# Decode attention on one core: Q loaded plainly and transposed on TensorE instead of by transposing DMAs, with a new fixed loop order and deeper buffers

## The chip, the cores and the metric

The kernel runs on one core of one Trainium2 chip. The metric is the device time of one execution in microseconds (us), lower being better. Each execution also has a span (first to last instruction) and the mean clock that TensorE was granted. Most executions of one kernel agree within about 0.3%, except for a rare slow state in which the granted clock is far lower; such a run is left out of comparisons.

## The reference

Grouped-query attention, with 4 query heads for each key/value head, all in bf16:

```python
B, Hq, Hkv, Sq, Sk, D = 16, 32, 8, 16, 2048, 128      # q: B,Hq,Sq,D   k, v: B,Hkv,Sk,D
k = jnp.repeat(k, 4, axis=1)
v = jnp.repeat(v, 4, axis=1)
scores = jnp.einsum("bhqd,bhkd->bhqk", q, k) * D ** -0.5
p = softmax(scores, axis=-1)
return jnp.einsum("bhqk,bhkd->bhqd", p, v)
```

For each of the 128 groups (one batch, one key/value head) 64 query rows meet 2048 keys. K and V are 67 MB each, and each byte is used for one group only, so the loads weigh about as much as the computing.

## The kernel before

Two groups make a *pair* (2 x 64 = 128 query rows), and the kernel is one unrolled pipeline over 64 pairs. For a pair p:

- SyncE issues loads of K and V (512 KB a group, rows of 4 KB to each partition), of Q, and the store of an earlier pair.
- TensorE (PE) transposes K in four blocks of eight 128x128 tiles (`KT`), each into one of three staging banks of PSUM (`ST_ps`); a copy (`kte`) takes each bank to SBUF.
- PE computes the scores (`S`) into `S_ps`, of which there is one; VectorE (DVE) scales them, takes the maximum and moves them to SBUF (`max`); ScalarE (ACT) does the exponential (`exp`).
- PE transposes P in two blocks (`PT`), copies (`pte`) take them out, PE multiplies by V (`PV`), and a last pass divides by the row sum (`norm`).

Each engine's program is a list made in Python. The parts that the change and the argument touch:

```python
NBK = 8; NBV = 12; NBO = 8      # slots for K, V and the output
DV = 2; DSTORE = 7              # V is issued 2 pairs after K, the store 7
QCH = 512                       # query rows in one load of Q: 16 loads

for kk in range(0, last_std + 1):                 # PE
    if kk < NP:  pe_prog.append(("S", kk))
    if kk >= 1:  pe_prog.append(("PT", kk - 1))
    pe_kt(kk)                                     # all four blocks of K of pair kk + 2
    if kk >= 1:  pe_prog.append(("PV", kk - 1))
# ... DVE: recip(kk-1), max(kk), all four K copies of pair kk + 2
# ... ACT: both P^T copies of kk-1, exp(kk), norm(kk-1)
# ... the last three pairs have an order of their own (`tail`)

def issue_q(c):
    sp.dma_start_transpose(QT[:, qch * c:qch * (c + 1)],
                           qf[qch * c:qch * (c + 1), :]).then_inc(sem_q[c], 16)

def issue_k(g):
    s = g % NBK
    if g >= NBK:                                  # slot free once its transposes are done
        ld = kt_loads[((g - NBK) // 2, (g - NBK) % 2, 1)]
        sp.wait_ge(sem_stage, ld["u"] + 1)
    sp.dma_start(Kn[s][:, :, :], k[b, h].rearrange("(a j) d -> a j d", j=J)).then_inc(sem_k[s], 16)

# PE, before transposing K: a load is there when all 16 increments are
pe.wait_ge(sem_k[s], 16 * (g // NBK + 1))
```

## Time and profile before

| before | value |
|---|---|
| median of the 12 runs beside the result | 380.04 us (379.74 to 380.91) |
| span of the profiled run, granted clock | 378.6 us, 0.995 |
| busy: PE, VectorE, ScalarE | 325.3, 307.9, 272.6 us |
| bytes moved by the queue of loads and stores | 138.43 MB |
| turn (start of one maximum to the next), steady | 5.60 us |

The columns are line, engine, operation, output and input, count; then busy time and mean nanoseconds; then the idle time just ahead of these instructions and what ended it.

```profile
L374 DVE TENSOR_SCALAR_CACHE_REDUCE Sneg<-S_ps 128x2048 f32<-128x2048 f32 x64 | 146.7, 2291 | 55.1 <-PE S_ps L312 55.1
L364 DVE COPY KT<-ST_ps 128x1024 bf16<-128x1024 bf16 x254 | 157.9, 683 | 7.9 <-PE ST_ps L300 7.7
```

VectorE stands idle for 55.1 us ahead of its maxima, waiting for scores: 64 x 0.86 us, the hole in each turn. It hardly waits for K's transposes (7.9 us).

### The profile page before, as it was taken

What the parts mean: (1) busy time and instruction counts of PE and PEld (TensorE: products, weight loads), DVE (VectorE), ACT (ScalarE), POOL (GpSimd) and SP (SyncE); (2) the same over time, 40 slices, a digit from 0 to 9 for tenths busy, and PEclk for the clock granted to TensorE, in tenths of its full rate; (3) what the DMA queues carried; (4) which work ended last, traced back from release to release, by engine and by line L of the source; (5) the groups of instructions that cost most, each with busy time, mean ns of one, the idle gap of its engine ahead of it and who ended that gap; (6) DMA issues with size and microseconds to landing.
All of it is one profiled execution on the core that took longest, in us unless ns stands there. A gap on an engine that the chain in (4) does not pass through costs nothing.

```text
span 378.6 us, 12914 instructions
## 1 busy us (share of the span) xinstructions
PE 325.3 (86%) x5632; PEld 257.0 (68%) x5632; DVE 307.9 (81%) x453; ACT 272.6 (72%) x316; POOL 1.0 (0%) x6
## 2 busy tenths in 40 slices
PE   4779889889888988988889889888988988988884
PEld 3567667677676776776677676776776776776664
DVE  2968888888898898797888898898898887898675
ACT  1457877777787787686877787787787786787882
POOL 1000000000000000000000000000000000000000
PEclk9989999999999999999999999999999999999999
DMA  8999999999999999999999999999999999999950
GB/s 256 346 407 345 407 404 351 410 346 409 355 399 413 345 402 347 410 406 346 412 344 407 366 394 408 348 412 348 406 411 346 406 342 412 406 409 409 409 204 12
DMA packets 54839, 139.25 MB, mean 368 GB/s; under 512 B 22016, under 2 KB 22016, under 8 KB 54784
## 3 DMA queue, kind: packets, MB, share of 16 engines
q1 hardware_dynamic: 54784, 138.43, 100.4%
q8 instruction: 45, 0.74, 0.8%
q14 instruction: 10, 0.08, 0.1%
HBM read 134.22 MB, written 2.10 MB: 360 GB/s over the span
## 4 chain that ended last, share of the span: by engine, by line
PE 54%; ACT 29%; DMA 9%; issue 3%; SPq 2%; DVE 1%
ACT PT L394 28%; PE O_ps L343 16%; PE ST_ps L300 16%; PE S_ps L312 13%; DMA Kn<-in_k_dram 9%; PE ST_ps L328 9%; SPq L234 1%; SPq L243 1%; DVE PT L364 1%; ACT KT L394 1%; DVE Sneg L374 0%; SPq L251 0%; DVE O L385 0%
## 5 line engine op out<-in xcount | busy, mean ns | idle before, releaser
L374 DVE TENSOR_SCALAR_CACHE_REDUCE Sneg<-S_ps 128x2048 f32<-128x2048 f32 x64 | 146.7, 2291 | 55.1 <-PE S_ps L312 55.1
L300 PE MATMUL ST_ps<-ident,Kn 128*128 128x128 bf16 x2048 | 147.1, 221 | 44.0 <-ACT PT L394 33.1
L394 ACT ACTIVATE PT<-ST_ps 128x1024 bf16<-128x1024 bf16 x124 | 120.1, 1021 | 66.1 <-PE ST_ps L328 66.1
L364 DVE COPY KT<-ST_ps 128x1024 bf16<-128x1024 bf16 x254 | 157.9, 683 | 7.9 <-PE ST_ps L300 7.7
L300 PEld LDWEIGHTS ST_ps<-ident,Kn 128*128 128x128 bf16 x2048 | 119.5, 99 | 65.4 <-issue 31.0
L398 ACT ACTIVATE P<-Sneg,nbias 128x2048 bf16<-128x2048 f32 x64 | 128.2, 2003 | 10.9 <-DVE Sneg L374 10.9
L328 PEld LDWEIGHTS ST_ps<-ident,P 128*128 128x128 bf16 x1024 | 57.4, 98 | 26.5 <-issue 25.2
L343 PE MATMUL O_ps<-Vb,PT 128*64 128x128 bf16 x2048 | 70.5, 222 | 4.6 <-ACT PT L394 1.9
L328 PE MATMUL ST_ps<-ident,P 128*128 128x128 bf16 x1024 | 68.5, 220 | 0.5 <-ACT KT L394 0.4
L343 PEld LDWEIGHTS O_ps<-Vb,PT 128*64 128x64 bf16 x2048 | 59.9, 111 | 11.9 <-DVE PT L364 2.6
L312 PE MATMUL S_ps<-KT,QT 128*64 128x512 bf16 x512 | 66.1, 379 | 1.9 <-DVE KT L364 1.0
L409 ACT ACTIVATE O<-O_ps,rrec 128x128 bf16<-128x128 f32 x61 | 22.4, 368 | 21.1 <-PE O_ps L343 21.1
L312 PEld LDWEIGHTS S_ps<-KT,QT 128*64 128x64 bf16 x512 | 25.9, 110 | 15.2 <-issue 2.4
L398 ACT ACTIVATION_READ_ACCUMULATOR P<-Sneg,nbias 128x1 f32 x64 | 12.8, 200 | 0.0
L368 DVE RECIPROCAL rrec<-rowsum 128x1 f32<-128x1 f32 x64 | 9.8, 154 | 3.2 <-ACT P L398 3.2
L374 DVE DVE_READ_ACCUMULATOR Sneg<-S_ps 128x1 f32 x64 | 5.3, 83 | 0.0
L385 DVE TENSOR_SCALAR O<-O_ps,rrec 128x128 bf16<-128x128 f32 x3 | 1.0, 349 | 2.5 <-PE O_ps L343 2.5
L394 ACT ACTIVATE KT<-ST_ps 128x1024 bf16<-128x1024 bf16 x2 | 1.9, 1020 | 1.3 <-PE ST_ps L300 1.3
L364 DVE COPY PT<-ST_ps 128x1024 bf16<-128x1024 bf16 x4 | 2.6, 686 | 0.1
L398 ACT ACT_TABLE_LOAD x1 | 1.3, 1283 | 0.7 <-PEq L424 0.7
L229 POOL TENSOR_SCALAR ident<-iota_t 128x128 bf16<-128x128 int32 x1 | 0.5, 536 | 0.1
L227 POOL IOTA iota_t<- 128x128 int32 x1 | 0.2, 235 | 0.4 <-POOLq L424 0.4
(4 smaller groups left out, 0.4 us busy)
## 6 DMA issues: line engine op xcount, KB each, us to landing
Kn<-in_k_dram SPq DMA_DIRECT2D x128, 512.0 KB, 13.0
Vb<-in_v_dram SPq DMA_DIRECT2D x128, 512.0 KB, 12.8
out_dram<-O SPq DMA_DIRECT2D x64, 32.0 KB, 12.6
QT<-in_q_dram SPq DMA_TRANSPOSE x16, 12.3
```

The lines of the kernel that those rows point to most:

```text
L234: sp.dma_start_transpose(QT[:, qch * c:qch * (c + 1)], qf[qch * c:qch * (c + 1), :]).then_inc(sem_q[c], 16)
L243: sp.dma_start(Kn[s][:, :, :], k[b, h].rearrange("(a j) d -> a j d", j=J)).then_inc(sem_k[s], 16)
L300: ins = pe.transpose(stage_ap(ld["bank"], t), Kn[s][:, j, :], ident[:, :])
L312: ins = pe.matmul(S_ps[64 * gg:64 * (gg + 1), 512 * c:512 * (c + 1)], QT[:, 128 * p + 64 * gg:128 * p + 64 * (gg + 1)], kt[:, gg, 4 * c:4 ...
L328: ins = pe.transpose(stage_ap(ld["bank"], t), P[p % 2][:, 128 * j:128 * (j + 1)], ident[:, :])
L343: ins = pe.matmul(O_ps[64 * gg:64 * (gg + 1), 0:128], pt[:, j, 64 * gg:64 * (gg + 1)], Vb[g % NBV][:, j, :], start=(j == 0), stop=(j == J ...
L364: dve.tensor_copy(evac_dst(ld), stage_bank_ap(ld["bank"])).then_inc(sem_ev["dve"], 1)
L368: dve.reciprocal(rrec[:, p:p + 1], rowsum[:, p:p + 1]).then_inc(sem_rec, 1)
L374: dve.tensor_scalar(Sneg[kk % 2][:, :], S_ps[:, :], -scale, None, op0=ALU.mult, op1=ALU.min, accum_out=nbias[:, kk:kk + 1],).then_inc(sem_ ...
L394: act.activation(evac_dst(ld), stage_bank_ap(ld["bank"]), ACT.Copy).then_inc(sem_ev["act"], 1)
L398: act.activation(P[kk % 2][:, :], Sneg[kk % 2][:, :], ACT.Exp, bias=nbias[:, kk:kk + 1], scale=-1.0, accum_out=rowsum[:, kk:kk + 1],).then ...
L409: act.activation(Osb[s_][:, :], O_ps[:, 0:128], ACT.Copy, scale=rrec[:, p:p + 1]).then_inc(sem_nm["act"], 1)
```

## The change

The intent: take the transposing loads away from the DMA engines, which are full, and put the work on PE and ScalarE, which are not; and order the loop so that VectorE's own work sets its turn. The diff, cut to its core:

```diff
-NBK = 8;  NBV = 12; NBO = 8;  DV = 2; DSTORE = 7; QCH = 512
+NBK = 12; NBV = 16; NBO = 12; DV = 3; DSTORE = 9; QCH = 1024; NPT = 2
+    for p in range(-4, NP + 4):
+        if (p + 2) % 8 == 0 and (p + 2) // 8 < NP // 8:
+            put(pe, "QT", (p + 2) // 8)
+        put(pe, "KT", p, 0)
+        put(pe, "PV", p - 3)
+        put(pe, "KT", p + 1, 1)
+        put(pe, "PT", p - 2)
+        put(pe, "S", p)
+        put(dve, "pte", p - 2, 1)
+        put(dve, "max", p)
+        put(dve, "recip", p - 1)
+        put(dve, "kte", p + 2, 1, 0)
+        put(dve, "kte", p + 2, 1, 1)
+        put(dve, "pte", p - 1, 0)
+        put(act, "exp", p)
+        if (p + 4) % 8 == 0 and (p + 4) // 8 < NP // 8:
+            put(act, "qte", (p + 4) // 8)
+        put(act, "kte", p + 2, 0, 0)
+        put(act, "kte", p + 2, 0, 1)
+        put(act, "norm", p - 1)
 ... (the old lists and the special tail are gone; exp also waits for the transposes of P two pairs back)
             def issue_q(c):
-                sp.dma_start_transpose(QT[:, qch * c:qch * (c + 1)], qf[qch * c:qch * (c + 1), :]).then_inc(sem_q[c], 16)
+                if c >= 2:
+                    sp.wait_ge(sem_stage, q_loads[c - 2]["u"] + 1)
+                sp.dma_start(Qn[c % 2][:, :, :], qf[qch * c:qch * (c + 1), :].rearrange("(a j) d -> a j d", j=8)).then_inc(sem_q[c], 16)
 ... PE:
+                elif op[0] == "QT":
+                    pe.wait_ge(sem_q[c], 16)
+                    wait_bank_free(ld)
+                    for t in range(8):
+                        ins = pe.transpose(stage_ap(ld["bank"], t), Qn[c % 2][:, t, :], ident[:, :])
 ... ScalarE copies that bank into QT with a strided view
```

## The prediction

> **What bounds the kernel now.** I read the page's busy table first. Nothing computing is full.
>
> ```profile
> PE 325.3 (86%) x5632; PEld 257.0 (68%) x5632; DVE 307.9 (81%) x453; ACT 272.6 (72%) x316; POOL 1.0 (0%) x6
> ```
>
> VectorE needs 307.9 us, 70 us less than the span, so a sum of work on one of these engines is not what sets the end. Next the queue table and the slices:
>
> ```profile
> DMA  8999999999999999999999999999999999999950
> GB/s 256 346 407 345 407 404 351 410 346 409 355 399 413 345 402 347 410 406 346 412 344 407 366 394 408 348 412 348 406 411 346 406 342 412 406 409 409 409 204 12
> ...
> q1 hardware_dynamic: 54784, 138.43, 100.4%
> ```
>
> The DMA engines are full from the first slice to the 38th; 138.43 MB pass in that time. But the rate is not steady: it is 402 to 413 GB/s in one slice and about 345 in the next. Cutting the span into 6 us windows (last two columns: DMA share, GB/s) shows what the dips are:
>
> ```profile
> 298.00:304.00 6.00, 5.67 (x98) 4.30 (x95) 5.03 (x10) 4.55 (x6) 0.00 (x0) 1.00 1.02 406
> 304.00:310.00 6.00, 5.05 (x89) 4.04 (x90) 5.16 (x10) 4.68 (x7) 0.00 (x0) 1.00 1.14 306
> ...
> 322.00:328.00 6.00, 5.39 (x97) 4.36 (x97) 5.16 (x9) 4.68 (x6) 0.00 (x0) 1.00 1.04 412
> 328.00:334.00 6.00, 5.39 (x99) 4.36 (x96) 5.16 (x9) 4.68 (x6) 0.00 (x0) 1.00 1.03 408
> ```
>
> About one window in four falls to some 306 to 325 GB/s while its DMA share rises: the engines take longer over fewer bytes. The Q chunks come at the same rate, one per four pairs, and the last dip (304 to 310) lies a queue's latency after the last one is issued at 297.6 us; behind it the rate stays at 408 to 412.
>
> ```profile
> Kn<-in_k_dram SPq DMA_DIRECT2D x128, 512.0 KB, 13.0
> ...
> QT<-in_q_dram SPq DMA_TRANSPOSE x16, 12.3
> ```
>
> So one transposing load of Q costs (409 - 309) / 409 x 6 = 1.45 us of all 16 engines. Checked on the whole: 138.43 MB at 409 GB/s is 338.5 us; the stream runs from about 2.2 to 364.4 us, 362.2 us; the surplus of 23.7 us over 16 transposes is 1.48 us each. Both ways agree.
>
> The second bound is the compute loop. The chain of waits is mostly compute:
>
> ```profile
> PE 54%; ACT 29%; DMA 9%; issue 3%; SPq 2%; DVE 1%
> ACT PT L394 28%; PE O_ps L343 16%; PE ST_ps L300 16%; PE S_ps L312 13%; DMA Kn<-in_k_dram 9%; PE ST_ps L328 9%; SPq L234 1%; SPq L243 1%; DVE PT L364 1%; ACT KT L394 1%; DVE Sneg L374 0%; SPq L251 0%; DVE O L385 0%
> ```
>
> and the timeline of VectorE in the middle shows its turn:
>
> ```profile
> 200.73 2.29 DVE L374 TENSOR_SCALAR_CACHE_REDUCE Sneg<-S_ps 128x2048 f32<-128x2048 f32 x1 [0.84 <-PE S_ps L312]
> 202.94 0.08 DVE L374 DVE_READ_ACCUMULATOR Sneg<-S_ps 128x1 f32 x1
> 202.94 2.48 DVE L364 COPY KT<-ST_ps 128x1024 bf16<-128x1024 bf16 x4
> 205.34 0.15 DVE L368 RECIPROCAL rrec<-rowsum 128x1 f32<-128x1 f32 x1
> 206.33 2.29 DVE L374 TENSOR_SCALAR_CACHE_REDUCE Sneg<-S_ps 128x2048 f32<-128x2048 f32 x1 [0.84 <-PE S_ps L312]
> ```
>
> A pair takes 206.33 - 200.73 = 5.60 us, with 0.84 us in which VectorE waits for the scores. The ring behind it, added up from the chain in order of time: two P^T evictions on ScalarE 1.95, hand-over 0.14, the second half of the K transposes 1.05, P·V 1.01, scores 0.86, first P transposes 0.57, hand-over 0.02: 5.60. The DMA needs 362.2 / 64 = 5.66 us per pair. Two limits stand within 1% of each other, and removing either alone would win little. Last come 14.2 us of tail, from the end of the loads (364.4) to the end (378.6).
>
> **What the Trainium skill says.** "DMA: Bandwidth & Descriptors", section "Latency and other measured facts", gives the DMA transpose 261 GB/s, 350 to 400 when contiguous. This trace does not agree: a Q chunk is 131 KB, worth 0.32 us at 409 GB/s, and took 0.32 + 1.45 us, some 74 GB/s. The same page, section "iDMA fabric", has a load stream of 4 KiB rows on a core alone at 408.7 GB/s; the undisturbed windows show 406 to 412, so I take 409 as the ceiling. "TensorE: Matmul & The Clock Gate", section "PE-mode transpose", says that the transpose leaves its result in PSUM and needs a copy after it; in the trace eight K transposes are issued in 0.45 us and each bank costs a copy of 683 ns on VectorE or 1021 ns on ScalarE. "PSUM — Partial Sum Buffer", section "PSUM bank collisions raise a hardware error", asks that a bank be guarded by semaphores against write and read at once; this is why an eviction's engine and place decide when PE goes on, and the wait list has PE waiting 33.1 us for ScalarE's P^T evictions.
>
> **The change part by part.** Q's load: 16 transposing DMAs become 8 plain ones with 2 KB per partition, of the same bytes. Gone: 16 x 1.48 = 23.7 us of DMA. New: 8 x 8 PE transposes, 8 x 0.45 = 3.6 us of PE, and 8 evictions, 8 x about 1.0 = 8 us of ScalarE, which has over 100 us idle; both lie beside other work. DMA per pair becomes 138.43 / 64 = 2.163 MB at 409 GB/s = 5.29 us.
>
> The loop: K's evictions are split evenly, two on VectorE and two on ScalarE, and P^T's both go to VectorE. Counts per pair on each engine do not change; order does. Floor of VectorE: maximum 2.22, reciprocal 0.1, four copies at 2.48 / 4 = 0.62: 4.80 us. ScalarE: exp 2.1, two copies 1.94, norm 0.37, 1/8 of Q's copy: 4.5. PE, issue alone: scores 1.0, P transposes 0.9, K transposes 1.8, P·V 0.9: 4.6. Walking the new order with the maximum of pair p starting at 0 and VectorE never waiting: PE ends its scores at -0.1, transposes half of K to 0.8, does P·V to 1.7 and the other half of K; its first bank is readable at 2.3, just as VectorE comes free (2.32). ScalarE empties the earlier K banks at 1.6 and 2.6, in time for PE at 2.15 and 2.6; P's transposes end at 3.55 (the second bank waits for VectorE's copy, to 3.1), the next scores are readable at 4.65, and VectorE is ready at 4.80. So the turn is 4.8 to 4.95 us, VectorE's own work, against 5.60. That is below the 5.29 of DMA: DMA becomes the only bound.
>
> Buffers: K's 12 slots and V's 16 let loads run some four and a half pairs, 9.7 MB, ahead; before, about 5.3 MB (13.0 us at 409) were in flight and kept the engines full. I expect no starvation. First scores come later, near 10 us instead of 8.6; the loop's 0.3 to 0.4 us a pair over DMA repays this well within 64 pairs.
>
> The end: loads 2.2 + 338.5 = 340.7. The last K lands 8 transfers earlier (V lags by three pairs): 8 x 0.524 / 409 = 10.3 us, so at 330.4. From there: first transposed bank 0.7; four copies 2.5 and small waits 0.3, then maximum 62 at 3.5 and done at 5.7; scores 63 readable 6.9; maximum 63 at 7.0; exp at 9.4; P transposes at 11.5; two copies, done 13.5; P·V with its hand-over 1.2; norm 0.4; store to the end 1.95 (before: 376.66 to 378.6): 17.1. V's last lands at 10.3 in this count, before it is needed. Span 330.4 + 17.1 = 347.5. The measured time is 1.4 over the span (380.0 against 378.6): 348.9. I add 1 us for the start and for leftover waits: **350 us**.
>
> **The rivals.** (1) The loop still sets the pace, because three staging banks and one scores buffer make a wait that my walk missed. For it: three engines at 4.5 to 4.8 us in a 5.3 us turn, hand-overs of 0.1 to 0.2 us at each step, Q's extra bank every eighth turn. Each 0.1 us over 5.29 costs 6.4 us; a turn of 5.6 would give about 10 + 63 x 5.6 + 12 + 1.4 = 376. Against it: 0.3 us of slack, and the walk closes. (2) The dips are not the transposes' own, or 2 KB rows of Q cost as much: then DMA keeps 362 us and the time is near 371. Against it: the clean last 50 us. (3) DMA starves at the start or behind in-order store waits (a store waits for a norm, and K loads stand behind it): plus 3 to 8 us. (4) Downwards: 412 GB/s instead of 409 is 2.5 us less, a shorter tail 2 more: 345.
>
> **Range and chances.** Most weight on a DMA-bound run, 346 to 353; some 12% on rival 1 or 3 with 355 to 366; few per cent on no gain. Range 345 to 356. Faster 0.96, within 2% 0.03, slower 0.01.
>
> **What would show it.** Right: slices flat at 405 to 412 GB/s without dips until about 340 us; turns of 5.3 us in the timeline; PE waiting for K loads, these heading the chain of waits; VectorE idle near 0.4 us a turn; about 7 us from last load to end. Wrong: dips that remain (rival 2); a DMA share below 0.95 with the queue waiting for buffers, and turns set by a ring of evictions (rival 1); holes in the first slices (rival 3).

## The result, and the profile after

The changed kernel takes **355.96 us** (median of 8 runs, 355.66 to 356.12) against 380.04 beside it: 24.1 us less. The ratio is 0.9364, 95% interval 0.9355 to 0.9373. A ratio here is the mean time of one kernel's fast runs over that of the other's of the same rounds, so it is not quite the ratio of the medians. The profiled run, at clock 1.0, has a span of 354.0 us. It is faster, as predicted, but 6 us above the point predicted (350), and it stands at the upper edge of the range of 345 to 356, which three of the eight runs exceed. That it lies inside is luck: it is outside the 346 to 353 that had most weight, where the prediction expected only its rivals 1 or 3, and neither of these came true.

The page first: busy times, slices, the queue of loads and stores and that of instructions, and the chain that ended last, by engine and by line.

```profile
PE 326.7 (92%) x5696; PEld 259.9 (73%) x5696; DVE 306.7 (87%) x448; ACT 276.4 (78%) x329; POOL 1.0 (0%) x6
DMA  7999999999999999999999999999999999999971
GB/s 291 414 408 407 407 405 411 411 411 408 410 411 411 411 409 409 411 410 410 411 411 409 410 410 408 412 412 410 411 406 406 411 410 411 408 412 404 389 279 29
q1 hardware_dynamic: 47232, 138.43, 98.6%
q8 instruction: 46, 0.75, 0.9%
DMA 47%; PE 46%; ACT 2%; DVE 1%; SPq 1%; issue 1%; DVEq 0%
DMA Kn<-in_k_dram 46%; PE ST_ps L294 18%; PE ST_ps L329 10%; PE S_ps L313 8%; PE O_ps L344 8%; ACT KT L400 2%; DMA Qn<-in_q_dram 1%; PE ST_ps L302 1%; SPq L240 1%; DVE Sneg L377 1%; ACT P L406 1%; DVE PT L367 1%; DVEq L218 0%; ACT O L417 0%; DVE rrec L371 0%
```

The same 138.43 MB, but no dips: 404 to 414 GB/s from the second slice to the 37th. Busy times are nearly those of before. The chain is headed by the loads of K, 46% against 9% before. Note the slices near the end, 404, 389 and 279: the stream does not end sharply but thins out. That is where the missing 6 us will be found.

Now VectorE's groups, with the same columns as before:

```profile
L377 DVE TENSOR_SCALAR_CACHE_REDUCE Sneg<-S_ps 128x2048 f32<-128x2048 f32 x64 | 146.3, 2287 | 2.3 <-PE S_ps L313 1.1
L367 DVE COPY KT<-ST_ps 128x1024 bf16<-128x1024 bf16 x128 | 82.7, 686 | 39.3 <-PE ST_ps L294 39.2
```

The 55.1 us of waiting for scores is 2.3. In its place are 39.3 us of waiting for K's transposes, which wait for loads. VectorE's timeline shows both kinds of turn; first one that no load holds up (start, length, engine, line, operation; idle time before it and its releaser in brackets):

```profile
89.31 2.29 DVE L377 TENSOR_SCALAR_CACHE_REDUCE Sneg<-S_ps 128x2048 f32<-128x2048 f32 x1
91.52 0.09 DVE L377 DVE_READ_ACCUMULATOR Sneg<-S_ps 128x1 f32 x1
91.52 0.16 DVE L371 RECIPROCAL rrec<-rowsum 128x1 f32<-128x1 f32 x1
91.87 1.29 DVE L367 COPY KT<-ST_ps 128x1024 bf16<-128x1024 bf16 x2 [0.19 <-PE ST_ps L294]
93.07 1.28 DVE L367 COPY PT<-ST_ps 128x1024 bf16<-128x1024 bf16 x2
94.27 2.28 DVE L377 TENSOR_SCALAR_CACHE_REDUCE Sneg<-S_ps 128x2048 f32<-128x2048 f32 x1
```

A free turn is 94.27 - 89.31 = 4.96 us, with 0.19 us idle. Then, from a turn that is held up, PE's line and the copy of VectorE behind it:

```profile
198.31 1.07 PE L294 MATMUL ST_ps<-ident,Kn 128*128 128x128 bf16 x16 [1.28 <-DMA Kn<-in_k_dram]
...
198.97 1.29 DVE L367 COPY KT<-ST_ps 128x1024 bf16<-128x1024 bf16 x2 [1.53 <-PE ST_ps L294]
```

PE waits 1.28 us for a load of K, and VectorE 1.53 us for PE. Free and held turns together give a mean of (343.51 - 13.53) / 63 = 5.24 us from the first maximum to the last, the DMA's pace. That is the shape predicted. What was not predicted shows in 6 us windows toward the end (busy time of PE, PEld, DVE, ACT, POOL with counts; granted clock; DMA share; GB/s):

```profile
306.00:312.00 6.00, 6.00 (x102) 4.67 (x102) 5.75 (x9) 5.22 (x6) 0.00 (x0) 1.00 1.03 409
330.00:336.00 6.00, 5.91 (x119) 4.76 (x117) 5.66 (x8) 5.06 (x7) 0.00 (x0) 1.00 1.03 380
336.00:342.00 6.00, 5.89 (x113) 4.75 (x108) 5.53 (x10) 5.04 (x7) 0.00 (x0) 1.00 0.86 328
342.00:348.00 6.00, 4.38 (x97) 3.37 (x94) 4.87 (x8) 4.70 (x7) 0.00 (x0) 1.00 0.38 134
```

The mean share of the 16 engines falls to 0.86, then to 0.38: some have run out of work while others still have it. The trace has the separate completion of each of the 16 engines' shares of a load. From these I computed when the first engine, the mean engine and the last engine were done; this is not a view of the profile, so it stands in an ordinary fence.

```
                 last K (group 127)          last V (group 127)
                 first   mean   last         first   mean   last engine, us
before           356.0  356.8  357.6         363.8  364.6  365.3
after            327.8  331.9  336.4         339.2  342.9  346.7

mean gap from first to last engine, after, in stretches of 40 us from 40 to 360 us:
2.3  3.6  4.7  5.6  6.9  7.9  8.2  8.6 us            (before: never over 1.7)
```

In the kernel before, the engines finish a load together, within 0.2 us, just after a transposing load of Q (12 of the 14 from 14 us on); then single engines fall back by some 1.6 us, at times when a packet of the instruction queue passes (16 KB, 1.07 us each; I call it a *fetch*, since these packets bring the program's instructions). The correspondence is exact: in each of the 13 stretches between two transposing loads from 14.3 to 309.6 us, as many engines are 1.5 to 1.7 us behind at the end as 16 KB fetches have passed (two or three), and as many 0.7 to 1.1 us behind as packets of 8 KB from the second instruction queue (none to two). The stores, about four in a stretch, set no engine back. In the changed kernel nothing brings them together again, the gap grows through the whole run, and every load is complete only with its slowest engine. Nothing in the chain of waits says this; it names only "DMA Kn".

The tail, from PE's and VectorE's and ScalarE's timelines:

```profile
336.46 0.90 PEld L294 LDWEIGHTS ST_ps<-ident,Kn 128*128 128x128 bf16 x16 [0.27 <-DMA Kn<-in_k_dram]
...
343.51 2.29 DVE L377 TENSOR_SCALAR_CACHE_REDUCE Sneg<-S_ps 128x2048 f32<-128x2048 f32 x1
...
345.85 2.00 ACT L406 ACTIVATE P<-Sneg,nbias 128x2048 bf16<-128x2048 f32 x1 [0.93 <-DVE Sneg L377]
...
350.15 1.08 PE L344 MATMUL O_ps<-Vb,PT 128*64 128x128 bf16 x32 [0.93 <-DVE PT L367]
351.27 0.37 ACT L417 ACTIVATE O<-O_ps,rrec 128x128 bf16<-128x128 f32 x1 [2.65 <-PE O_ps L344]
```

The last K is transposed from 336.46 (the line shows the weight loads of it, waiting for the load), the last maximum begins at 343.51, its exponential at 345.85, the last P·V at 350.15, and the last store ends the span at 354.0. From K's landing that is 17.6 us. The last V (346.7) lands before its P·V needs it.

### The profile page after: what moved, and what is told of

It reads as the page before. It is cut to its first block, busy times and chain, and to the rows that moved or that the text cites. A ratio compares the mean times of both kernels' runs of the same rounds, so it can differ in the third digit from the quotient of the medians.

```text
span 354.0 us, 13113 instructions
## 1 busy us (share of the span) xinstructions
PE 326.7 (92%) x5696; PEld 259.9 (73%) x5696; DVE 306.7 (87%) x448; ACT 276.4 (78%) x329; POOL 1.0 (0%) x6
## 3 DMA queue, kind: packets, MB, share of 16 engines
q1 hardware_dynamic: 47232, 138.43, 98.6%
## 4 chain that ended last, share of the span: by engine, by line
DMA 47%; PE 46%; ACT 2%; DVE 1%; SPq 1%; issue 1%; DVEq 0%
DMA Kn<-in_k_dram 46%; PE ST_ps L294 18%; PE ST_ps L329 10%; PE S_ps L313 8%; PE O_ps L344 8%; ACT KT L400 2%; DMA Qn<-in_q_dram 1%; PE ST_ps L302 1%; SPq L240 1%; DVE Sneg L377 1%; ACT P L406 1%; DVE PT L367 1%; DVEq L218 0%; ACT O L417 0%; DVE rrec L371 0%
## 5 line engine op out<-in xcount | busy, mean ns | idle before, releaser
L400 ACT ACTIVATE KT<-ST_ps 128x1024 bf16<-128x1024 bf16 x128 | 124.0, 1021 | 57.5 <-PE ST_ps L294 57.5
L294 PE MATMUL ST_ps<-ident,Kn 128*128 128x128 bf16 x2048 | 138.0, 221 | 13.2 <-DMA Kn<-in_k_dram 9.6
L294 PEld LDWEIGHTS ST_ps<-ident,Kn 128*128 128x128 bf16 x2048 | 116.2, 98 | 44.4 <-issue 23.7
L367 DVE COPY KT<-ST_ps 128x1024 bf16<-128x1024 bf16 x128 | 82.7, 686 | 39.3 <-PE ST_ps L294 39.2
L367 DVE COPY PT<-ST_ps 128x1024 bf16<-128x1024 bf16 x128 | 81.9, 681 | 0.9 <-PE ST_ps L329 0.9
L329 PE MATMUL ST_ps<-ident,P 128*128 128x128 bf16 x1024 | 71.1, 220 | 1.2 <-ACT KT L400 0.4
L329 PEld LDWEIGHTS ST_ps<-ident,P 128*128 128x128 bf16 x1024 | 59.7, 98 | 5.8 <-issue 2.2
L400 ACT ACTIVATE QT<-ST_ps 128x1024 bf16<-128x1024 bf16 x8 | 8.2, 1024 | 12.8 <-PE ST_ps L302 12.8
L406 ACT ACTIVATION_READ_ACCUMULATOR P<-Sneg,nbias 128x1 f32 x64 | 13.5, 210 | 0.0
L302 PE MATMUL ST_ps<-ident,Qn 128*128 128x128 bf16 x64 | 5.3, 231 | 6.9 <-DMA Qn<-in_q_dram 6.9
L302 PEld LDWEIGHTS ST_ps<-ident,Qn 128*128 128x128 bf16 x64 | 3.9, 102 | 9.8 <-issue 9.8
## 6 DMA issues: line engine op xcount, KB each, us to landing
Kn<-in_k_dram SPq DMA_DIRECT2D x128, 512.0 KB, 13.3
Vb<-in_v_dram SPq DMA_DIRECT2D x128, 512.0 KB, 13.5
Qn<-in_q_dram SPq DMA_DIRECT2D x8, 256.0 KB, 12.4
```

Of the source, the lines that this page charges most:

```text
L294: ins = pe.transpose(stage_ap(ld["bank"], t), Kn[s][:, j, :], ident[:, :])
L302: ins = pe.transpose(stage_ap(ld["bank"], t), Qn[c % 2][:, t, :], ident[:, :])
L329: ins = pe.transpose(stage_ap(ld["bank"], t), P[p % 2][:, 128 * j:128 * (j + 1)], ident[:, :])
L367: dve.tensor_copy(evac_dst(ld), stage_bank_ap(ld["bank"])).then_inc(sem_ev["dve"], 1)
L400: act.activation(evac_dst(ld), src, ACT.Copy).then_inc(sem_ev["act"], 1)
L406: act.activation(P[kk % 2][:, :], Sneg[kk % 2][:, :], ACT.Exp, bias=nbias[:, kk:kk + 1], scale=-1.0, accum_out=rowsum[:, kk:kk + 1],).then ...
```

## The experiments

My theory after the result: the gain is that of the prediction, loads without stops feeding a faster loop, and the missing 6 us is an imbalance of the 16 DMA engines, set by instruction fetches and formerly wiped out at each transposing load (the *fetch theory*). Its rivals: the loop or its buffers still hold the loads back (the *loop rival*), or the engines are made uneven by something else, such as the stores (the *stores rival*). The ten runs were made in three lots, each on one chip with its own runs of the kernel before, whose medians were 379.98, 380.09 and 380.03 us. Times are compared with the changed kernel's 355.96, which came back as 355.93.

### The new loop with the old transposing loads

```diff
-QCH = 1024
+QCH = 512
-        if (p + 2) % 8 == 0 ...: put(pe, "QT", (p + 2) // 8)      # and "qte" on ScalarE
-                sp.dma_start(Qn[c % 2][:, :, :], qf[...].rearrange("(a j) d -> a j d", j=8)).then_inc(sem_q[c], 16)
+                sp.dma_start_transpose(QT[:, qch * c:qch * (c + 1)], qf[qch * c:qch * (c + 1), :]).then_inc(sem_q[c], 16)
```

> The changed kernel with its new loop, its larger buffers and its new store order, but with Q loaded by the 16 transposing DMAs of before. If the transposes are what holds the DMA stream (my step: 1.48 us each, 23.7 us in all), the stream ends near 362 us again, the 145 to 345 GB/s dips return, and the time is near 371 us (last K at 352, tail of 17.6, 1.4 over the span). I also expect the spread between the first and the last of a transfer's 16 completion increments to be pulled back below 2 us at each transpose, as in the kernel before, instead of growing to 9 us. Rival: if the loop's order alone made the gain, the time stays within 2 us of the changed kernel's 356.

Measured: three fast runs of 373.5 to 373.9 us, ratio 0.9833 (0.9815 to 0.9851); near 371 was expected. Its profiled run fell in the slow state (448.39 us at clock 0.661) and is not used. The kernel was therefore sent again for one look:

> The same kernel as e1_transposing_q, whose profile fell into a slow state (granted clock 0.661); this run is for a profile at full clock. Expected: 373.8 us, dips of the DMA rate at each of the 16 transposes, turns of the loop of 4.96 us where K is there, last K's slowest engine near 353 to 355 us, spread below 2 us throughout.

That run took 373.87 us at clock 0.991, span 372.0. Its state is formally unknown, being a single run, but it agrees with the three fast ones. Its slices:

```profile
GB/s 250 356 406 338 410 355 395 409 343 412 347 408 411 341 406 354 403 413 346 406 348 408 392 361 410 344 411 355 397 407 351 409 341 405 410 406 412 407 410 80
```

The dips are back. The gap of the engines is at most 1.8 us in the loads of K and V, and the stream ends sharply (410, then 80). The last V lands at 365.2, where it landed before (365.3). So the new loop with its deeper buffers gains 6.2 us alone, and all of it in the tail: from the last V to the end it needs 372.0 - 365.2 = 6.8 us, against 378.6 - 365.3 = 13.3.

Against the changed kernel this isolates Q's loads. The *mean* engine is done with the last K at 353.9 here and at 331.9 there: 22.0 us, close to the 23.7 predicted. The *slowest* engine is done at 354.8 and 336.4: 18.4 us. The measured times differ by 373.87 - 355.96 = 17.9 us. The difference of the first two, 3.6 us, is what the lost alignment took back.

### The old loop with plain loads of Q

```diff
 (from before)
-QCH = 512
+QCH = 1024
+        if (kk + 2) % 8 == 0 and (kk + 2) // 8 < NP // 8:
+            pe_prog.append(("QT", (kk + 2) // 8))            # after PV
+            act_prog.append(("qte", (kk + 2) // 8))          # after norm
-                sp.dma_start_transpose(...)
+                sp.dma_start(Qn[c % 2][:, :, :], qf[...].rearrange("(a j) d -> a j d", j=8)).then_inc(sem_q[c], 16)
```

> The kernel before with its loop, buffers and tail, but with the plain loads of Q and PE transposes (8 of them). If the old loop's turn of 5.60 us is a second bound, the turns stay at 5.60 us, the DMA stream no longer sets the pace (its share falls under 1, about 386 GB/s in the middle), and the time is near 372 us: 380 less the waits for K in the middle (about 2.5 us) and at the start (about 5 us). Rival: if Q's transposes were the only bound, this alone gives 356 to 360 us.

Measured: 382.82 us, ratio 1.0074 (1.0056 to 1.0092). A clear miss of mine, by 11 us: freeing the DMA makes the old kernel slightly *slower*, though its last V lands at 356.1, 9 us earlier. VectorE's timeline, an ordinary turn and one with Q's transposes in it:

```profile
269.79 2.29 DVE L400 TENSOR_SCALAR_CACHE_REDUCE Sneg<-S_ps 128x2048 f32<-128x2048 f32 x1 [0.84 <-PE S_ps L336]
...
275.39 2.29 DVE L400 TENSOR_SCALAR_CACHE_REDUCE Sneg<-S_ps 128x2048 f32<-128x2048 f32 x1 [0.84 <-PE S_ps L336]
...
281.67 2.29 DVE L400 TENSOR_SCALAR_CACHE_REDUCE Sneg<-S_ps 128x2048 f32<-128x2048 f32 x1 [1.51 <-PE S_ps L336]
```

The old loop keeps its 5.60 us turn with 0.84 us idle whatever the DMA does; a turn with Q in it is 6.28. The starts of all 64 maxima, compared with those of before, give the whole sum: before had 2.5 us of turns over 5.60 in the middle and one of 8.66 at the start (3.1 over), which are gone; the first maximum comes 3.2 us later (12.88 against 9.68); and seven turns are longer by 0.68 us, 4.8 in all. 378.6 - 2.5 - 3.1 + 3.2 + 4.8 = 381.0, and the span is 381.1. The engines' gap rises to 5.1 us here and falls back to about 2 from 190 us on: in this run, where the loads are not the bound, the engines catch up. Together with the run before this fills a table of the two parts:

| | old loop | new loop, deeper buffers |
|---|---|---|
| transposing loads of Q | 380.0 | 373.8 (-6.2) |
| plain loads, PE transposes | 382.8 (+2.8) | 356.0 (-24.0) |

Each part alone gives 6 us or less; together they give 24. This is what two bounds side by side look like. No run separates the new order from the deeper buffers and the later V and stores.

### Fewer instruction fetches

PE's stream is cut by doing only part of the transposes of P and of P·V from the fourth pair on. The output is wrong; the loads are unchanged.

```diff
-                        for t in range(8):              # transposes of P
+                        for t in range(8 if p < 3 else 1):
-                    for j in range(J):                  # P·V
+                    for j in range(J if p < 3 else 1):
```

> The changed kernel with about half of PE's instructions left out (P.V with one key block of 16 and the P transposes that feed it; a wrong result on purpose); all loads, all evictions, VectorE and ScalarE work stay. Theory: the last 6 us over my prediction come from the instruction fetches (46 of 16 KB), which share some of the 16 DMA engines, so that these fall behind the others (9 us at the end) and every load lands with its slowest engine. With 24 fetches instead of 46 the spread should be about half, 4.5 to 5 us at the end, the last K should land near 333 us instead of 336.4, and the time be near 351 (3.5 us from the DMA, about 1.5 from a shorter tail). Rival A: the DMA rate of plain loads is simply 2% lower than I took, whatever the instructions: the last K still lands near 336 and only the tail's 1 to 2 us are gained. Rival B: the compute loop's late start is what costs: the last K moves by less than 1 us.

Measured: 350.22 us, ratio 0.9213. The granted clock was 0.89 to 0.95, where no other fast run is below 0.98. The page's instruction queue:

```profile
q8 instruction: 25, 0.41, 0.5%
```

25 fetches instead of 46. The last K's mean engine is done at 330.5 instead of 331.9: 1.4 us, and 21 fetches x 1.07 us / 16 engines is 1.4. Its slowest engine is done at 332.7 instead of 336.4, and the gap mean-to-slowest is 2.2 us instead of 4.5. Not every measure is halved: from first to last engine the gap of this load is 5.6 us instead of 8.6, and for the last V it is 7.1 against 7.5, after a fetch at 338.8 us set the slowest engine back by another 1.5 us. The span falls by 5.4 us: 3.7 from the landing and 1.7 from a tail of 15.9 instead of 17.6, since the last pair has less to do. This speaks for the fetch theory. But it removes PE's work along with its instructions, so alone it does not settle that the fetches do it; hence the next run.

### More instruction fetches

GpSimd, idle otherwise, gets waits that are fulfilled at once: more instructions, and no work. The expectation speaks of 4000 waits; the kernel that ran has 8000.

```diff
+            for _ in range(8000):
+                gp.wait_ge(sem_id, 1)
```

> The changed kernel with 4000 waits on an already reached semaphore value added to the idle POOL engine: about 250 KB of instructions more, some 15 fetches of 16 KB on top of 46. If fetches are what makes DMA engines lag, the spread at the end rises from 9 us (about a third more if they fall on the same engines: 12 us), the last K lands about 3 us later, and the time is near 358 to 359. If POOL's fetches fall on other engines than PE's, the spread stays and only the mean rises (15 x 1.07 / 16 = 1 us): about 356.5. Rival: if fetches cost nothing, 356.0 as before.

Measured: 366.68 us, ratio 0.9645 (0.9632 to 0.9658), 10.7 us slower than the changed kernel; I had expected 2 to 3. The queue that carries these fetches and the slices:

```profile
GB/s 301 407 409 406 407 406 408 410 409 408 410 410 408 411 408 390 411 400 396 399 401 407 400 403 360 401 394 403 390 382 399 402 375 395 394 404 386 376 189 19
...
q14 instruction: 41, 0.34, 0.2%
```

There were 10 such packets in the changed kernel, so 31 more came, of 8 KB each: only 0.26 MB, about the bytes expected. Yet the last V lands at 358.3 (slowest engine) instead of 346.7. The completions show why the effect is that large: nine of these packets, some 11.4 us apart from 43.7 to 134.8 us, each set the *same* engine back by 0.6 to 1.0 us. From about 140 us on this one engine stands 8 to 9 us behind the first, and from about 180 us on the other 15 are within 3 us of each other. At about 9 us the gap stops growing and the rate of the whole stream falls (slices of 360 to 404): from there on all loads go at the pace of that one engine. Why the gap has this ceiling was not tested. Counted to the slowest engine, some 12 to 14 transfers are under way in this run; what limits them may be what holds the fast engines back. So fetches alone, without any work, unbalance the engines and cost time. The direction confirms the fetch theory, and the size shows that it is the share of one engine that counts, not the bytes in all.

### Stores on eight engines

This is the stores rival. Every second store is given a shape that only eight engines carry (the trace shows eight completions for it instead of 16, and one more mark at its issue). Rows come out permuted.

```diff
+                dst = of[128 * p:128 * (p + 1), :]
+                if p % 2:
+                    dst = dst.rearrange("(b a) d -> a b d", a=8)
```

> The changed kernel with every second store written through a row-permuted view whose slowest dimension is 8 (rows of odd pairs come out permuted: a wrong result on purpose, the same bytes). By the Trainium skill, DMA: Bandwidth & Descriptors, section on why a DMA increments its semaphore by 16, such a copy runs on 8 engines, the lowest-numbered. Stores cost 18 ns per 256-byte packet, so this moves 32 x 128 x 18 ns / 16 = 4.6 us of work off each of eight engines onto each of the other eight. If engine imbalance is what delays the end and the fetches sit on the upper eight, the spread at the end falls from 9 to near 1 us and the time to about 352; if the fetches sit on the lower eight, the spread rises to about 18 us and the time to about 360. Rival: if the imbalance is not what delays the end, the time stays within 1 us of 356.

Measured: 357.6 us (two runs at 356.8, two at 358.4 and 358.77; the profile is of one of the faster), ratio 0.9411; the last K at 336.9. The gap fell to about 7 us, but by the first engines' finishing later and not by the last ones' finishing earlier. Neither expectation came true, and the run is inconclusive: which engines carry the fetches stays open. What speaks against the stores is the count of fetches in the kernel before, above.

### Small transposing loads beside plain Q

Does the old cost follow from the bytes that are transposed? The changed kernel gets 16 transposing loads of 32 KB, a quarter of the old ones, into an unused tile, one per four pairs.

```diff
+                    if nk % 8 == 2:
+                        c = nk // 8
+                        sp.dma_start_transpose(scratch[:, 128 * c:128 * (c + 1)], qf[128 * c:128 * (c + 1), :]).then_inc(sem_x, 16)
```

> The changed kernel with 16 transposing DMAs of 32 KB each (128 rows of Q into a scratch tile that nobody reads) put back at the rate of before, one per four pairs. It measures the transpose's cost apart from Q's bytes. If each costs by its bytes, a quarter of 1.48 us, the stream gets 16 x 0.37 = 6 us longer (time about 362, less what the realigned engines give back). If the cost is a stop of all engines that hardly depends on size, each costs near 1.2 to 1.5 us and the time is 370 to 374. In both cases the spread should be pulled below 2 us at each transpose.

Measured: 376.57 us, ratio 0.9905 (0.9892 to 0.9919), above both expectations. The slices:

```profile
GB/s 286 406 344 404 347 405 407 348 411 348 404 411 347 411 342 408 402 356 408 344 408 361 395 408 347 409 352 404 412 343 407 346 404 407 349 408 349 407 411 58
```

(376.57 - 355.96) / 16 = 1.29 us each, at a quarter of the bytes (0.08 us of it is for the bytes, which are extra here); the 131 KB loads cost (373.87 - 355.96) / 16 = 1.12 us each by the same subtraction. So a transposing load costs a stop of all engines, hardly by its size. The engines' gap is again at most 1.7 us: the stop also realigns them. That is shown apart from Q, since Q itself is loaded plainly here.

The packets and completions show what the stop is made of. At each of the 14 transposing loads from 14.3 us on in the kernel before, 18 to 21 packets are held, most of them for about 1.4 us, and all are let go within 0.2 us of each other, when the slowest engine has come up. Over such a load the slowest engine loses 0.5 to 0.7 us (12 of the 14; 0.32 of it is the bytes at 409 GB/s), the fastest about 2.0. In this run, with 32 KB, it is 0.3 to 0.4 and about 1.9 us. Just ahead of it the slowest stands 1.2 us behind the mean. So most of the 1.48 us is the other engines' waiting for the one that a fetch has set back: the kernel before pays for the imbalance at every stop, the changed kernel once, at the end. Whether a transposing load is cheap where nothing has set an engine back was not run.

### V later

If K decides the end and V does not, then issuing V later lets the last K land earlier. One number is changed.

```diff
-DV = 3
+DV = 5
```

> The changed kernel with V's loads five pairs behind K's instead of three; nothing else. In the changed kernel the end is the last K (336.4 us at its slowest engine) plus a chain of 17.6 us, while the last V lands at 346.7 and has only P.V, norm and the store behind it. With five pairs of lag the last K should land some 5 us earlier (331) and its chain end at 349; the last V stays at 346.7, plus 1.1 + 0.4 + 2.0 = 350.3: the span about 350.5 and the time about 352, 1% less. Rival: the loads then run only some two and a half pairs ahead, the DMA engines run dry in places and the time stays at 356 or rises.

Measured: 359.45 us, ratio 0.9453 (0.944 to 0.9466), 3.5 us slower where 4 us less was expected. The loads did as expected: last K at 331.2 (336.4 before it), last V at 346.9. The chain and one row of the waits (waiting, releaser: total us, count, largest) name what I had overlooked:

```profile
DMA Vb<-in_v_dram 29%; PE ST_ps L294 24%; PE O_ps L344 15%; PE S_ps L313 12%; PE ST_ps L329 12%; SPq L240 2%; SPq L248 1%; DVE Sneg L377 1%; PE ST_ps L302 1%; DVE PT L367 1%; SPq L231 0%; DVEq L218 0%; ACT O L417 0%; DVE rrec L371 0%
...
PE O_ps L344 <- DMA Vb<-in_v_dram: 8.6, 12, 1.4
```

In PE's order the P·V of pair p - 3 stands ahead of pair p's scores. A later V holds up that P·V, and with it the scores behind it. The last maximum starts at 346.97 instead of 343.51 though its K landed 5 us earlier. V's delay has to be matched by a later P·V.

### V and P·V later

```diff
-NPT = 2
+NPT = 3
-DV = 3
-DSTORE = 9
+DV = 5
+DSTORE = 11
-    for p in range(-4, NP + 4):
+    for p in range(-4, NP + 6):
-        put(pe, "PV", p - 3)
+        put(pe, "PV", p - 5)
-        put(act, "norm", p - 1)
+        put(act, "norm", p - 3)
```

> What e4 got wrong was that P.V stands before the scores of a later pair in PE's order, so a later V held up the scores. Here V's loads lag by five pairs and P.V and norm too (P.V of pair p-5 in turn p, norm two turns later, three P^T buffers, stores two steps later); all else as in the changed kernel. Then the last K (331.2 us at its slowest engine in e4) is followed by its chain with nothing of V in it: P.V of the last pair could start at 331.2 + 13.6 = 345, and waits for the last V (346.9); with 1.1, 0.4 and 2.0 after it the span is about 350.5 and the time about 352, 1% under the changed kernel. Rival: the end is set by the loop's backlog and not by the order of the loads, so the time stays at 356 or above.

Beside it, on the same chip, the changed kernel once more:

> The changed kernel itself, unaltered, for the comparison on the same chip and in the same rounds: 356.0 us, ratio 0.936 to the kernel before; the spread at the end again near 9 us, last K near 336 us, last V near 347 us.

Measured: **353.07 us** (352.75 to 353.17), ratio 0.9285 (0.9267 to 0.9304), correct; the changed kernel beside it 355.93, ratio 0.936 (0.9341 to 0.9379). So it is 2.9 us faster than the changed kernel, and the fastest that computes the right result; 352 was expected. Last K at 331.1, last V at 346.7 (slowest engines). Its end:

```profile
346.96 1.08 PE L344 MATMUL O_ps<-Vb,PT 128*64 128x128 bf16 x32 [0.55 <-ACT O L417]
348.08 0.37 ACT L417 ACTIVATE O<-O_ps,rrec 128x128 bf16<-128x128 f32 x1 [1.27 <-PE O_ps L344]
```

The last P·V starts at 346.96, released by the norm ahead of it, and only 0.3 us after the last V landed. So the chain from the last K and the landing of the last V now end nearly together; shifting V further was not tried. The changed kernel repeated its landings to 0.1 us for K (336.4) and 0.0 for V (346.7), so the imbalance is not an accident of one run.

## Why the prediction was right or wrong

- **Two bounds within 1% of each other: right.** The table of the two parts shows it: -6.2 and +2.8 us alone, -24.0 together.
- **The cost of a transposing load, 1.45 to 1.48 us of all engines: right in size, not in its make-up.** The dips are gone with the loads, come back with them, and come with 32 KB too. Rival 2 is out. By the mean engine 16 of them are worth 22.0 us instead of 23.7. (The first sum, (409 - 309) / 409 x 6, is 1.47.) That some 1.2 us of each is a wait for the slowest engine was not seen.
- **The loop: right.** A free turn was predicted at 4.8 to 4.95 us and measures 4.96; the DMA's turn at 5.29, and the mean is 5.24. VectorE's idle time per turn follows (39.3 / 64 = 0.6 us ahead of K's copies, predicted near 0.4). Q's transposes do not "lie beside other work": a turn with them takes 5.62 us, 0.66 more than a free one. At one turn in eight this is 0.08 us a turn, and the mean stays at the DMA's pace. Rival 1 is out.
- **The buffers: not shown.** The prediction has loads run "9.7 MB, ahead". A load of K still takes 13.3 us from issue to landing, against 13.0 before, so no more bytes are under way than before; no run has the new loop with the old buffers.
- **The start: wrong, without consequence.** The first scores begin at 12.4 us (8.6 before), not near 10, and the first maximum at 13.53. The loads did not wait for it: the second slice already has 414 GB/s. Rival 3 is out too.
- **The tail: right.** From the last K: last maximum 7.0 predicted and 7.1 measured, exponential 9.4 and 9.4, P's transposes done 11.5 and copies 13.5 against P·V starting at 13.7; 17.1 in all, measured 17.6. From the last V to the end 354.0 - 346.7 = 7.3, predicted about 7.
- **The loads' end: this step failed.** "So at 330.4" for the last K, by way of "loads 2.2 + 338.5 = 340.7". Measured are 331.9 for the mean engine, 1.5 late, and 336.4 for the slowest, another 4.5 late. The mechanism, loads without stops, was right and the size was off in one term: the "16 x 1.48 = 23.7 us of DMA" that would be gone were worth 17.9 us in time, because the stops had also been keeping the 16 engines together. The prediction treated the engines as one pipe of 409 GB/s; none of its rivals had 16 pipes, the slowest of which counts. The Trainium skill says what should have led there: "DMA: Bandwidth & Descriptors", section "Why a DMA increments its semaphore by 16 and not by 1", has the engines finish independently and a load complete only at the full 16. The trace agrees, with up to 9.16 us between the first and the sixteenth.
- **The sum.** 336.4 + 17.6 = 354.0 of span, and the median time is 1.96 more, where 1.4 was taken: 355.96 (the profiled run itself took 355.88). Six late microseconds at the last K, 0.5 in the tail and 0.6 outside the span make 7.1; the 1 us of allowance covered part of it, and about 6 remain.

That fetches set the imbalance rests on three things: in the kernel before exactly one engine falls back for each fetch, with 25 fetches instead of 46 the last K lands 3.7 us earlier, and fetches without work make a gap and cost 10.7 us. The loop rival is out: the slices are flat at 404 to 414 GB/s to the 37th. The stores rival is out by the count of fetches. It stays open which engines carry the fetches, why the gap grows at its particular pace, and why it stops near 9 us.

## What to carry to other kernels

When two limits stand within a per cent or two of each other, expect little from removing one, and price the two together. In a kernel that is bound by loads, look at when each of the 16 engines finishes a load, not only at the mean rate: the stream that thinned out at its end (404, 389, 279 GB/s) had uneven engines, and here the amount of code made them so. The transposing loads were dear mainly because the engines came to them uneven: look at what makes them uneven as well as at the stop. Last, what a late load holds up is decided by the place of its consumer in the engine's order: shift both or neither.

## What the Trainium skill lacked or had wrong

- "DMA: Bandwidth & Descriptors", section "Latency and other measured facts", gives the DMA transpose as a bandwidth, 261 GB/s or 350 to 400. Here a transposing load among plain ones costs 1.12 us (131 KB) and 1.29 us (32 KB) of the whole stream, so hardly by its bytes; the page doesn't say that the other transfers are held until the slowest engine has come up (packets held about 1.4 us), nor that the engines are level right after it (gap 0.2 us or less).
- The same page, section "Why a DMA increments its semaphore by 16 and not by 1", doesn't say how far apart the engines may be. Here the gap grows to 9.16 us in a run of 354 us, and the last K lands 4.5 us behind its mean engine.
- "Runtime: NRT & Kernel Launch", section "Instruction fetch mechanics", calls the cost of crossing a 16 KiB block "one DMA tail-bump, mostly hidden". The blocks agree (46 packets, 0.75 MB). The cost isn't hidden in a kernel bound by loads: 21 fetches fewer brought the last K 3.7 us earlier, and 31 more of 8 KB took 10.7 us.
